# Result rows on adjacent partitions, brought together from two PSUM banks by two engines, at the end of an attention decode kernel

## The chip, the cores and the metric

The kernel runs on one core of one Trainium2 chip. The metric is the device time of one execution in microseconds. Most executions agree within 0.3%; all runs compared here are of the fast (undisturbed) state. The profile's span, from the first to the last instruction, is some 1.5 us shorter than that time. A page prints the span to 0.1 us; where hundredths are used below, they come from the trace itself (244.59 us before).

## The reference, cut to what matters

Two independent decode steps, A and B, each with one query token, 32 query heads, 16 key/value heads, head size 128. A attends to the last 2048 positions of its cache, B to all 8192. Each multiplies the joined heads (4096 values) with an output matrix `wo` and yields 576 numbers; the results are joined.

```python
def _B_ref(x, k_cache, v_cache, wq, wo):          # _A_ref: the same on the last 2048 positions
    q = (x @ wq).reshape(B, Sq, Hq, Dh).transpose(0, 2, 1, 3)
    k = jnp.repeat(k_cache, rep, axis=1)
    v = jnp.repeat(v_cache, rep, axis=1)
    p = _softmax(jnp.einsum("bhqd,bhkd->bhqk", q, k) * (Dh ** -0.5))
    o = jnp.einsum("bhqk,bhkd->bhqd", p, v)
    return o.transpose(0, 2, 1, 3).reshape(B, Sq, Hq * Dh) @ wo
# result: jnp.concatenate([a, b], axis=-1), 2 x 576 numbers in bf16
```

## The kernel before

Only the last step matters here. `wo` lies in SBUF as 32 rows of 576 columns on each of 128 partitions; the sum over 32 matmul steps, each contracting 128 partitions, gives the result. The 576 columns are dealt out over column groups of 32: two groups with 288 columns for A, four with 144 for B. Each group writes its own 32 PSUM partitions, of which one row is the result.

```python
DM = 576
OUTS = [2, 4]                       # column groups of A and of B
opj = nc.alloc_sbuf_tensor("opj", [128, 2, 64], BF16)         # columns 32.. are zero
outsb = nc.alloc_sbuf_tensor("outsb", [128, 2, DM // 2], BF16)
# ... ktps[0..3]: PSUM banks 0 to 3, 128 x 512 f32
def o_columns(P):
    add("dve", lambda dve: dve.tensor_copy(opj[:, P, 0:32], wsum[:, 272 + 32 * P:304 + 32 * P]),
        reads=[B_W], writes=[("opj", P)])
# ...
def wo_part(P, lo, n, off, res):
    def mm(pe):
        for jj in range(lo, lo + n):
            w = DM // OUTS[P]
            for j in range(OUTS[P]):
                o = off + (jj - lo) * DM + j * w
                ins = pe.matmul(ktps[P][32 * j:32 * j + 32, 0:w], lhsT=opj[:, P, jj:jj + 32],
                                rhs=slots[:, o:o + w], start=(jj == 0), stop=(jj == HQ - 1))
        return ins
    add("pe", mm, reads=[("opj", P)] + res, writes=[("bank", P)])

def finish_out(P):
    n = OUTS[P]
    add("dve", lambda dve: dve.tensor_copy(outsb[0:32 * n, P, 0:DM // n], ktps[P][0:32 * n, 0:DM // n]),
        reads=[("bank", P)], writes=[("outsb", P)])
    def put(eng):                   # n rows, 32 partitions apart
        src = bass.AP(tensor=outsb, offset=P * DM // 2, ap=[[32 * DM, n], [1, DM // n]])
        dst = out[0, 0:1, P * DM:(P + 1) * DM].rearrange("o (j n) -> (o j) n", j=n)
        return eng.dma_start(dst, src)
    add("sp", put, reads=[("outsb", P)], writes=[("out", P)], dma="out%d" % P)
# ... the last loads: wo of B in pieces of 21, 7, 3 and 1 rows; then for P in (0, 1): wo_part, finish_out
```

## Time and profile before

| | before |
|---|---|
| time, median of 3 (later of 6) | 246.19 (246.03) us |
| span | 244.6 us |
| bytes read | 102.76 MB at 420 GB/s |
| landings of the last two pieces of weights (3 rows, 1 row) | 241.87, 242.24 us |
| last matmul, copy, issue of the store end at | 242.56, 242.90, 243.49 us |

The kernel is a stream of loads with a serial tail. The prediction shows the lines of that tail, all but one: the weight loads of the last four matmuls wait once more, for the last row of weights.

```profile
242.29 0.10 PEld L690 LDWEIGHTS ktps<-slots,opj 128*32 128x32 bf16 x4 [0.19 <-DMA slots<-in_B_wo_dram]
```

The stretch after the last copy holds no instruction on a compute engine; it is read from windows of the trace. The columns are the stretch, its length, the busy time of the five engines, TensorE's clock, the share of the DMA engines' time that was busy, and GB/s. These are, of the kernel before: the issue of B's store (the time for which the profile shows its queue, `SPq` for SyncE, at work on it), the silence until its bytes, its bytes, and the rest to the end of the span.

```profile
242.92:243.50 0.58, 0.00 (x0) 0.00 (x0) 0.00 (x0) 0.00 (x0) 0.00 (x0) 1.00 0.00 0
243.50:244.13 0.63, 0.00 (x0) 0.00 (x0) 0.00 (x0) 0.00 (x0) 0.00 (x0) 1.00 0.00 0
244.13:244.22 0.09, 0.00 (x0) 0.00 (x0) 0.00 (x0) 0.00 (x0) 0.00 (x0) 1.00 0.08 13
244.22:244.59 0.37, 0.00 (x0) 0.00 (x0) 0.00 (x0) 0.00 (x0) 0.00 (x0) 1.00 0.00 0
```

The edges of windows are rounded to 0.01 us; by the trace the four take 0.57, 0.64, 0.09 and 0.36 us. From the start of the issue to the end of the span pass 1.66 us.

### The profile page before, as it was taken

Reading aid. Unit: us, or ns where it says so; the run is one execution under the profiler, and the core shown is the slowest. Engines: PE = TensorE matmul, PEld = TensorE weight load, DVE = VectorE, ACT = ScalarE, POOL = GpSimd, SP = SyncE. Lnnn points to the kernel's source line nnn. Section 1 sums busy time; section 2 is a strip of 40 time slices with the busy share of each in tenths; the row PEclk is TensorE's granted clock in tenths of the full one; section 3 lists DMA queues with packets and bytes.
Section 4 is the critical chain, followed back from the end, with each engine's and each line's share of the span. In section 5 each row is a group of like instructions: output and inputs, shape, how many; then the busy total and the mean of one; then the engine's idle time right before and its main releaser. Section 6 shows DMA issues by size and latency. Waiting matters only on the chain. (4 is left out here: it accounts for less than half of the span.)

```text
span 244.6 us, 5211 instructions
## 1 busy us (share of the span) xinstructions
PE 165.4 (68%) x2325; PEld 121.3 (50%) x2325; DVE 88.2 (36%) x152; ACT 92.7 (38%) x95; POOL 6.3 (3%) x33
## 2 busy tenths in 40 slices
PE   0007339968389995393999362999457799945965
PEld 0002139746236773233887221987232787624854
DVE  0001407864316454203556302455322246543031
ACT  2000016855306686102678300687600378630000
POOL 5000100000000000000000000000000000000000
PEclk9999957997759999569899859799957589975599
DMA  9999999999999999899999999999989999989993
GB/s 338 434 410 418 434 437 426 429 426 426 445 426 430 482 407 450 380 439 429 478 439 429 413 418 429 434 504 397 461 375 434 429 488 397 461 388 428 414 409 135
DMA packets 4068, 102.88 MB, mean 421 GB/s; under 512 B 602, under 2 KB 732, under 8 KB 988
## 3 DMA queue, kind: packets, MB, share of 16 engines
q1 hardware_dynamic: 3900, 102.76, 98.1%
q8 instruction: 6, 0.10, 0.2%
q10 hardware_dynamic: 160, 0.00, 0.0%
q14 instruction: 2, 0.02, 0.0%
HBM read 102.76 MB, written 0.00 MB: 420 GB/s over the span
## 5 line engine op out<-in xcount | busy, mean ns | idle before, releaser
L506 ACT ACTIVATE kt<-ktps 128x1024 bf16<-128x1024 bf16 x80 | 79.5, 1036 | 89.6 <-PE ktps L496 89.6
L496 PE MATMUL ktps<-ident,slots 128*128 128x128 bf16 x1280 | 87.8, 234 | 22.5 <-PEq L214 19.2
L496 PEld LDWEIGHTS ktps<-ident,slots 128*128 128x128 bf16 x1280 | 81.7, 106 | 38.0 <-issue 37.9
L509 DVE COPY kt<-ktps 128x1024 bf16<-128x1024 bf16 x80 | 60.7, 768 | 59.0 <-PE ktps L496 59.0
L588 PE MATMUL opsum<-slots,ptm 128*32 128x512 bf16 x320 | 28.5, 532 | 9.8 <-PEq L214 9.8
L521 PE MATMUL sacc<-kt,qst 128*32 128x512 bf16 x320 | 25.4, 392 | 2.2 <-PEq L214 2.2
L588 PEld LDWEIGHTS opsum<-slots,ptm 128*32 128x32 bf16 x320 | 14.0, 129 | 22.9 <-issue 20.6
L559 PE MATMUL misc<-ident,psb 128*128 128x128 bf16 x40 | 4.6, 285 | 15.8 <-PEq L214 15.8
L547 ACT ACTIVATE psb<-sacc,stat 128x2048 bf16<-128x2048 f32 x5 | 9.8, 1967 | 10.1 <-DVE stat L536 10.1
L606 DVE TENSOR_TENSOR vtmp<-opsum,maskV 128x512 f32<-128x512 f32 x4 | 2.8, 692 | 30.2 <-PE opsum L588 30.2
L559 PEld LDWEIGHTS misc<-ident,psb 128*128 128x128 bf16 x40 | 3.4, 125 | 18.2 <-issue 18.2
L438 PE MATMUL misc<-xnine,twice 64*128 64x18 bf16 x1 | 0.2, 170 | 18.0 <-DMA xnine<-in_B_x_dram 18.0
L566 DVE TENSOR_TENSOR ptm<-misc,maskP 128x1024 bf16<-128x1024 bf16 x5 | 3.5, 691 | 16.0 <-PE misc L559 16.0
L521 PEld LDWEIGHTS sacc<-kt,qst 128*32 128x32 bf16 x320 | 5.0, 94 | 8.3 <-issue 4.6
L438 PEld LDWEIGHTS misc<-xnine,twice 64*128 64x128 bf16 x1 | 0.1, 99 | 18.0 <-issue 18.0
L462 ACT ACTIVATE qrow<-opsum 128x512 bf16<-128x512 f32 x1 | 0.6, 597 | 19.4 <-PE opsum L456 19.4
L690 PE MATMUL ktps<-slots,opj 128*32 128x144 bf16 (+1 forms) x192 | 6.7, 247 | 0.7 <-issue 0.5
L690 PEld LDWEIGHTS ktps<-slots,opj 128*32 128x32 bf16 x192 | 5.3, 96 | 1.9 <-issue 0.6
L447 DVE TENSOR_SCALAR xpad<-misc,par 128x5 bf16<-128x5 f32 (+1 forms) x8 | 1.2, 229 | 13.8 <-PE misc L438 13.8
L481 POOL COPY qst<-qcol 128x32 bf16<-128x32 bf16 x8 | 1.7, 211 | 147.4 <-PE sacc L521 147.4
L559 PE MATMUL turned<-ident,psb 128*128 128x128 bf16 x40 | 5.3, 313 | 0.0
L534 DVE TENSOR_REDUCE stat<-sacc 128x1 f32<-128x512 f32 x5 | 3.5, 691 | 4.4 <-PE sacc L521 4.4
(75 smaller groups left out, 52.9 us busy)
## 6 DMA issues: line engine op xcount, KB each, us to landing
slots<-in_B_k_cache_dram SPq DMA_DIRECT2D x8, 4096.0 KB
slots<-in_A_k_cache_dram SPq DMA_DIRECT2D x4, 2048.0 KB
slots<-in_A_v_cache_dram SPq DMA_DIRECT2D x4, 2048.0 KB
slots<-in_A_wq_dram SPq DMA_DIRECT2D x1, 4608.0 KB, 13.8
slots<-in_B_wq_dram SPq DMA_DIRECT2D x1, 4608.0 KB, 24.0
slots<-in_A_wo_dram SPq DMA_DIRECT2D x1, 4608.0 KB, 18.7
slots<-in_B_wo_dram SPq DMA_DIRECT2D x1, 3024.0 KB, 25.5
slots<-in_B_wo_dram SPq DMA_DIRECT2D x1, 1008.0 KB, 7.7
```

Source lines behind the costliest of these rows:

```text
L481: return pool.tensor_copy(dst, src)
L496: ins = pe.matmul(ktps_bf[q][:, t * 128:(t + 1) * 128], lhsT=slots[:, o:o + 128], rhs=ident[:, :], start=True, stop=True, is_transpose=True)
L506: add("act", lambda act, src=src, dst=dst: act.activation(dst, src, ACT.Copy), reads=[("bank", q)], writes=[("kt", u % NKT, q)], tag="e%d% ...
L509: add("dve", lambda dve, src=src, dst=dst: dve.tensor_copy(dst, src), reads=[("bank", q)], writes=[("kt", u % NKT, q)], tag="e%d%d" % (u, q))
L521: ins = pe.matmul(sacc[32 * j:32 * j + 32, :], lhsT=qst[:, o:o + 32], rhs=rhs, start=(u == 0 and e == 0), stop=True, skip_group_check=True)
L534: add("dve", lambda dve: dve.tensor_reduce(st(C_M + g), sacc[:, :], AX.X, ALU.max), reads=[B_S], writes=[("st", C_M + g)], tag="max")
L547: return act.activation(dst, src, ACT.Exp, bias=st(C_NB + g), scale=SCALE, accum_out=st(C_L + g))
L559: ins = pe.matmul(dst[:, t * 128:(t + 1) * 128], lhsT=psb[:, o:o + 128], rhs=ident[:, :], start=True, stop=True, is_transpose=True)
L566: return dve.tensor_tensor(ptm[:, c * 1024:(c + 1) * 1024].rearrange("p (t y) -> p t y", t=8), dst.rearrange("p (t y) -> p t y", t=8), mas ...
L588: ins = pe.matmul(opsum[64 * j + 32 * x:64 * j + 32 * x + 32, :], lhsT=ptm[:, o:o + 32], rhs=v[:, at[0], at[1], :, :, b:b + 128], start=(n ...
L606: add("dve", lambda dve: dve.tensor_tensor(vtmp[:, :, :], src, by, ALU.mult), reads=[B_O, w], writes=["vtmp"], tag="keep")
L690: ins = pe.matmul(ktps[P][32 * j:32 * j + 32, 0:w], lhsT=opj[:, P, jj:jj + 32], rhs=slots[:, o:o + w], start=(jj == 0), stop=(jj == HQ - 1))
```

## The change

The intent is to let the store take two adjacent rows of 576 B in place of rows that lie 32 partitions apart. The result row of a column group falls on the partition that the place of the weight column in its 32-column window gives. The window of even groups is placed so that the result comes on the group's partition 31, that of odd groups so that it comes on the first, which is partition 32 of the pair. B has two such pairs of groups, each with half of a row's columns; the second pair writes another bank, and ScalarE copies it to partitions 31 and 32 while VectorE copies the first.

```diff
-    opj = nc.alloc_sbuf_tensor("opj", [128, 2, 64], BF16)
+    opj = nc.alloc_sbuf_tensor("opj", [128, 2, 96], BF16)
 ...
-        add("dve", lambda dve: dve.tensor_copy(opj[:, P, 0:32], ...
+        add("dve", lambda dve: dve.tensor_copy(opj[:, P, 31:63], ...
 ...
-                    o = off + (jj - lo) * DM + j * w
-                    ins = pe.matmul(ktps[P][32 * j:32 * j + 32, 0:w], lhsT=opj[:, P, jj:jj + 32],
+                    o = off + (jj - lo) * DM + j % 2 * (DM // 2) + j // 2 * w
+                    at = jj + j % 2 * 31
+                    ins = pe.matmul(ktps[P + j // 2][32 * j:32 * j + 32, 0:w], lhsT=opj[:, P, at:at + 32],
 ...
-        add("pe", mm, reads=[("opj", P)] + res, writes=[("bank", P)])
+        add("pe", mm, reads=[("opj", P)] + res, writes=[("bank", P + k) for k in range(P + 1)])
 ...
-        n = OUTS[P]
-        add("dve", lambda dve: dve.tensor_copy(outsb[0:32 * n, P, 0:DM // n], ktps[P][0:32 * n, 0:DM // n]),
-            reads=[("bank", P)], writes=[("outsb", P)])
- ... (put, shown above)
+        w = DM // OUTS[P]
+        for k, name in enumerate(("dve", "act")[0:P + 1]):
+            dst, src = outsb[0:64, P, k * w:(k + 1) * w], ktps[P + k][64 * k:64 * k + 64, 0:w]
+            add(name, lambda eng, k=k, dst=dst, src=src:
+                eng.activation(dst, src, ACT.Copy) if k else eng.tensor_copy(dst, src),
+                reads=[("bank", P + k)], writes=[("outsb", P, k)]).key = ("outsb", P)
+        add("sp", lambda sp: sp.dma_start(out[0, 0:1, P * DM:(P + 1) * DM].rearrange("o (j n) -> (o j) n", j=2),
+                                          outsb[31:33, P, :]),
+            reads=[("outsb", P, k) for k in range(P + 1)], writes=[("out", P)], dma="out%d" % P)
```

More of the change, by code (lines that the diff above doesn't have):

```diff
@@ L675, in o_columns @@
     def o_columns(P):
-        add("dve", lambda dve: dve.tensor_copy(opj[:, P, 0:32], wsum[:, 272 + 32 * P:304 + 32 * P]),
+        add("dve", lambda dve: dve.tensor_copy(opj[:, P, 31:63], wsum[:, 272 + 32 * P:304 + 32 * P]),
             reads=[B_W], writes=[("opj", P)])
@@ L688, in mm @@
                 for j in range(OUTS[P]):
-                    o = off + (jj - lo) * DM + j * w
-                    ins = pe.matmul(ktps[P][32 * j:32 * j + 32, 0:w], lhsT=opj[:, P, jj:jj + 32],
+                    o = off + (jj - lo) * DM + j % 2 * (DM // 2) + j // 2 * w
+                    at = jj + j % 2 * 31
+                    ins = pe.matmul(ktps[P + j // 2][32 * j:32 * j + 32, 0:w], lhsT=opj[:, P, at:at + 32],
                                     rhs=slots[:, o:o + w], start=(jj == 0), stop=(jj == HQ - 1))
             return ins
-        add("pe", mm, reads=[("opj", P)] + res, writes=[("bank", P)])
+        add("pe", mm, reads=[("opj", P)] + res, writes=[("bank", P + k) for k in range(P + 1)])
     def finish_out(P):
-        n = OUTS[P]
-        add("dve", lambda dve: dve.tensor_copy(outsb[0:32 * n, P, 0:DM // n], ktps[P][0:32 * n, 0:DM // n]),
-            reads=[("bank", P)], writes=[("outsb", P)])
-        def put(eng):
-            src = bass.AP(tensor=outsb, offset=P * DM // 2, ap=[[32 * DM, n], [1, DM // n]])
-            dst = out[0, 0:1, P * DM:(P + 1) * DM].rearrange("o (j n) -> (o j) n", j=n)
-            return eng.dma_start(dst, src)
-        add("sp", put, reads=[("outsb", P)], writes=[("out", P)], dma="out%d" % P)
+        w = DM // OUTS[P]
[7 more added lines that the diff above has]
+            reads=[("outsb", P, k) for k in range(P + 1)], writes=[("out", P)], dma="out%d" % P)
     WQ = [(4 * SLOT - WQ_W, [("v", 2)]), (SLOT, [("k", 1, 0), ("k", 1, 1), ("v", 0)])]
```

## The prediction

> **What bounds the kernel now.** I read the page's header and its part 2 first, to see which resource is full from end to end. Then the chain of waits over the last 20 us, which says what sets the end. Then the timeline of the last 2.5 us, because everything that the change edits lies there, and a few groups of instructions for durations.
>
> ```profile
> span 244.6 us, 5211 instructions
> ...
> PE 165.4 (68%) x2325; PEld 121.3 (50%) x2325; DVE 88.2 (36%) x152; ACT 92.7 (38%) x95; POOL 6.3 (3%) x33
> ...
> DMA  9999999999999999899999999999989999989993
> ...
> HBM read 102.76 MB, written 0.00 MB: 420 GB/s over the span
> ```
>
> The row DMA reads 9 (that is, 90% or more) or 8 in every slice but the last. No other engine is above 68%. The kernel streams 102.76 MB at 420 GB/s, and the transfers are the bound until the last weights have landed. Only the last slice (6 us) shows a 3: there the stream has run dry and a serial tail remains. The chain of waits gives the order of that tail (start, length, what):
>
> ```profile
> 233.52 8.35 DMA slots<-in_B_wo_dram
> 241.87 0.04 issue
> 241.92 0.65 PE ktps L690 x16
> 242.56 0.02 issue
> 242.59 0.31 DVE outsb L698
> ```
>
> The last four rows of B's output weights land at 241.87; 16 matmuls finish the sum by 242.56; one VectorE copy takes it out of PSUM. The timeline of the same stretch, and the one of A's result three microseconds earlier, show what follows a copy:
>
> ```profile
> 242.59 0.31 DVE L698 CAST outsb<-ktps 128x144 bf16<-128x144 f32 x1 [2.89 <-PE ktps L690]
> 242.92 0.57 SPq L704 DMA_DIRECT2D out_dram<-outsb  x1
> ```
> ```profile
> 239.25 0.45 DVE L698 CAST outsb<-ktps 64x288 bf16<-64x288 f32 x1 [3.62 <-PE ktps L690]
> 239.73 0.60 SPq L704 DMA_DIRECT2D out_dram<-outsb  x1
> ```
>
> B's copy ends at 242.59 + 0.31 = 242.90; SyncE takes up the store at 242.92 and is at it for 0.57 us, to 243.49. Windows of 0.05 us show the bytes of this store between 244.10 and 244.25, and the span ends at 244.6. So after the last matmul come 0.03 + 0.31 + 0.02 + 0.57 = 0.93 us of copying and issuing, about 0.61 us until the first bytes, some 0.15 us of bytes and some 0.35 us to the end: 2.04 us in all. That, plus at most the 0.65 us of matmuls, is all the change can reach: 2.7 of 244.6 us, 1.1%. A's store is issued 3.2 us before B's and is not on the path.
>
> The time outside is 246.19 us, 1.6 us more than the span; I carry that difference over unchanged.
>
> **What the Trainium skill says.** Four places bear on the edited operations.
>
> 1. "DMA: Bandwidth & Descriptors", section "Why a DMA increments its semaphore by 16 and not by 1": a store issued from SyncE uses the largest number of DMA engines up to 16 that divides the slowest dimension of both sides, and completion waits for each. B's store goes from four rows to two, so from four engines to two. The page of the kernel before does not list engines for this store, so nothing here confirms it.
> 2. Same page, "Latency and other measured facts": about 600 ns to the first byte for this kind of store. The trace agrees: 243.49 to 244.10 is 0.61 us. This part doesn't depend on the rows. The page's "Specifications" also says that pieces under 512 B cost a read-modify-write; the pieces grow from 288 B (144 elements of 2 B) to 576 B.
> 3. "ScalarE: Activation LUTs", section "What ACT_TABLE_LOAD costs": an activation with immediate scale and bias takes 186 ns + 0.833 ns per element of a row. For 512 elements that gives 612 ns; the trace has 597 for the 128x512 copy from PSUM, so it agrees to 3%. The section on table sets says that copies are in every set; the trace has a single table load of 1283 ns although copies and exponentials alternate, so no load of a table is to be feared.
> 4. "PSUM — Partial Sum Buffer", section "Specifications (TRN2)": ScalarE and VectorE may read PSUM side by side at full rate as long as their banks differ. The two copies read banks 1 and 2. No instruction of the kernel before shows two reads timed against each other, so I rely on the page here.
>
> **The change part by part.**
>
> The matmuls. The order of instructions on TensorE is the same in both kernels: 64 of 288 columns, 128 of 144 columns, each with a 32-column weight window. The window starts 31 columns later for odd column groups, which moves the result row from the group's first partition to partition 31 (even groups) or keeps it at the first (odd groups). Column groups 2 and 3 of B now write another bank. Nothing in count, size or wait changes: **0**.
>
> Clearing the weight buffer on GpSimd. 128x128 becomes 128x192. The 128x128 clear took 0.20 us and the 128x576 one 0.58, so 0.38 us per 448 columns, and 64 more columns cost about 0.05 us at 3.4 us into the run. TensorE's first matmul waits until 18.00 us for x by DMA and the work on VectorE that GpSimd releases is over at 4.4 us. Hidden: **0**.
>
> VectorE's copy for B. 128x144 becomes 64x144. The two old copies tell what a copy costs: both carry 18,432 elements, yet 64x288 took 450 ns and 128x144 took 307. So time goes by the columns (143 ns for 144 more, 0.99 ns each, on top of some 164 ns) and not by the partitions. Half the partitions save nothing: 307 ns remains, **0**.
>
> ScalarE's copy for B, new: 64x144 with partitions 64 to 127 as its source. From the page's formula 186 + 144 x 0.833 = 306 ns (an estimate). From this trace, between the 5-column activation of 208 ns and the 512-column copy of 597: 208 + 139 x 389/507 = 315 ns. From the copies of 512 and of 1024 columns (1036 ns): 597 - 368 x 0.857 = 282 ns. So 282 to 315 ns, side by side with VectorE's 307. ScalarE has been idle since 222.3 us, and took 0.03 us to react to VectorE there (222.10 to 222.13). It ends between 0.03 before and 0.01 us after VectorE: **0 to +0.02**. The split gains no copying time; it is there because two engines each bring one bank's half of each row to the same two partitions.
>
> The wait of SyncE. One semaphore counted to two by two engines instead of to one by VectorE. Reaction 0.02 us as before: **0**.
>
> The store of B. Two pieces of 576 B in place of four of 288 B. For the issue the trace has just these two forms: A's two pieces of 576 B took 0.60 us, B's four of 288 B took 0.57. B's store now has A's form, so the issue doesn't shrink: **-0.02 to +0.03**. The bytes: they are on the move for about 0.15 us, with staggered starts among engines; two engines in place of four, and no small pieces, may take 0 to 0.08 us off. The 0.35 us of receipt may shrink by up to 0.05 us because two completions have to come in and not four: together **-0.10 to 0**.
>
> The store of A has the same form (two pieces of 576 B), only from adjacent partitions, and is off the path: **0**.
>
> Sum: between -0.12 and +0.05 us, most likely -0.04. 246.19 - 0.04 = 246.15 us.
>
> **The rivals.**
>
> (a) *The split halves the copy.* If time went by elements, 0.31 us would become 0.16, and the kernel 246.03. Against it speak the two copies of equal element count above. For it: nothing.
>
> (b) *The small store was costly.* If a partial write of 288 B costs a read before the write, the bytes and receipt (0.5 us together) could lose 0.2 to 0.3 us: 245.9 to 246.0. For it: the page's 512 B. Against: the whole stretch from the first bytes to the end is 0.5 us, much of it fixed.
>
> (c) *ScalarE becomes the last.* It might start late, after 20 us of waiting outside its loop, or a read across partitions may be slow. At +0.1 to +0.3 us this makes 246.3 to 246.5. The reaction time of 0.03 us speaks against it; no earlier activation in the trace writes other partitions than it reads, so the doubt stays.
>
> (d) *The stream itself changes.* Other semaphores and a longer program could shift when loads start, and 1% of the stream is 2.4 us. But all loads stand in the same order behind the same waits, and everything edited but the clear comes after the last load was issued (234.4 us). I give it little.
>
> **Range and chances.** Every rival stays within 0.4 us, so the range is set by the repeat scatter, 245.87 to 246.22 in three runs of one kernel, plus the rivals: 245.7 to 246.6. A change beyond 2% is 4.9 us, nearly twice the 2.7 us that the edited tail lasts, so no mechanism of the change reaches it: faster 0.005, within 2% 0.99, slower 0.005.
>
> **What would show each step right or wrong.** The group of VectorE's copy at 64x144 should read 300 to 315 ns (rival a: 160 to 240), and ScalarE's new 64x144 row 280 to 320 ns, both starting within 0.05 us of the last matmul's end (rival c: ScalarE later or longer). The issue of B's store should take 0.55 to 0.62 us. From the end of issue to the end of the span should be 1.0 to 1.1 us, against 1.1 before; at 0.9 or less rival (b) is right. From the last matmul's end to the span's end should be 1.9 to 2.1 us. The landing of the last weights, which the change does not touch, may move by some tenths between any two runs, and that alone may decide the sign of the difference. A table load before ScalarE's copy, a gap in the row DMA before the last slice, or a time outside 244 to 248 us would prove my reading of the kernel wrong.

## The result, and the profile after

The changed kernel takes 245.47 us (median of 6 runs, 245.41 to 245.69), the kernel before 246.03 us in 6 runs (245.87 to 246.22). The ratio is 0.9978 with a 95% interval of 0.9966 to 0.9991. A ratio is the mean time of one kernel's fast runs over that of the other's fast runs of the same rounds, so it is not quite the ratio of the medians. The gain is 0.56 us of the medians: within 2%, but outside the predicted range of 245.7 to 246.6 us.

The page of the changed kernel, span and row of the DMA engines by slices:

```profile
span 244.0 us, 5212 instructions
...
DMA  9999999999999999899999999999989999989994
```

The stream is as full as before. The chain of waits of its last microseconds (start, length, what), and the timeline from the copies on:

```profile
231.89 9.93 DMA slots<-in_B_wo_dram
241.82 0.04 issue
241.87 0.64 PE ktps L691 x16
242.51 0.02 issue
242.53 0.30 DVE outsb L703
```
```profile
242.53 0.29 ACT L703 ACTIVATE outsb<-ktps 64x144 bf16<-64x144 f32 x1 [21.12 <-PE ktps L691]
242.53 0.30 DVE L703 CAST outsb<-ktps 64x144 bf16<-64x144 f32 x1 [4.46 <-PE ktps L691]
242.86 0.26 SPq L705 DMA_DIRECT2D out_dram<-outsb  x1
```

The landings (241.82 and 242.19 us against 241.87 and 242.24), the 16 matmuls (0.64 against 0.65) and the copy (0.30 against 0.31) hardly moved, and ScalarE's copy runs beside VectorE's. The last loads were released 1.6 us earlier in this execution than in the one before (231.89 against 233.52), and still landed at the same time, which fits DMA engines that are busy all the while (8 or 9 in the row DMA until the last slice). What moved is the issue of the store, from 0.57 to 0.26 us. The windows of the changed kernel, cut at the same events as those of before:

```profile
242.86:243.12 0.26, 0.00 (x0) 0.00 (x0) 0.00 (x0) 0.00 (x0) 0.00 (x0) 1.00 0.00 0
243.12:243.60 0.48, 0.00 (x0) 0.00 (x0) 0.00 (x0) 0.00 (x0) 0.00 (x0) 1.00 0.00 0
243.60:243.64 0.04, 0.00 (x0) 0.00 (x0) 0.00 (x0) 0.00 (x0) 0.00 (x0) 1.00 0.12 29
243.64:244.02 0.38, 0.00 (x0) 0.00 (x0) 0.00 (x0) 0.00 (x0) 0.00 (x0) 1.00 0.00 0
```

Line by line against before, by the trace's times: the issue -0.31 us, the silence after it -0.15, the bytes -0.05, the rest +0.01. Together 1.15 in place of 1.66 us: -0.51 us. With the 0.05 by which the last row landed earlier and 0.01 from there to the start of the issue it makes up the 0.57 us by which the spans differ.

The same shows in A's store, which is off the path: the prediction has it at 0.60 us in the kernel before; the changed kernel issued it in 0.29 us. A's store has two pieces of 576 B in both kernels. So neither the number nor the size of the pieces can be what made it quick, and the step between the rows became the theory to test. (The kernel before also writes its source pattern by hand, with `bass.AP`, where the changed kernel takes a slice; the first experiment rules that out.)

### The profile page after: what moved, and what is told of

It is laid out like the page before. It is cut to its first block, busy times and chain, and to the rows that moved or that the text cites. A ratio compares the mean times of both kernels' runs of the same rounds, so it can differ in the third digit from the quotient of the medians.

```text
span 244.0 us, 5212 instructions
## 1 busy us (share of the span) xinstructions
PE 165.8 (68%) x2325; PEld 120.5 (49%) x2325; DVE 88.2 (36%) x152; ACT 93.2 (38%) x96; POOL 6.4 (3%) x33
## 5 line engine op out<-in xcount | busy, mean ns | idle before, releaser
L588 PE MATMUL opsum<-slots,ptm 128*32 128x512 bf16 x320 | 27.4, 515 | 7.7 <-PEq L214 7.7
L588 PEld LDWEIGHTS opsum<-slots,ptm 128*32 128x32 bf16 x320 | 13.3, 125 | 20.3 <-issue 18.0
```

Of the source, the lines that this page charges most:

```text
L588: ins = pe.matmul(opsum[64 * j + 32 * x:64 * j + 32 * x + 32, :], lhsT=ptm[:, o:o + 32], rhs=v[:, at[0], at[1], :, :, b:b + 128], start=(n ...
```

## The experiments

Every experiment is the changed kernel with one edit, unless it says otherwise. They ran in three groups, each on a chip of its own, each beside runs of the kernel before: its medians there were 246.04, 246.03 and 246.06 us, so the three groups can be laid side by side.

**Theory S:** the partition step of the rows that the store reads sets how long its issue takes. **Rival P:** fewer and larger pieces. **Further questions:** what ScalarE and the second bank bring by themselves, and whether A's store counts.

### B's rows 32 partitions apart again

```diff
-                    at = jj + j % 2 * 31
+                    at = jj + 31 - ROWS[P][j % 2]          # B: rows 31 and 63; A: 31 and 32
 ...
-                                          outsb[31:33, P, :]),
+                                          bass.AP(tensor=outsb, offset=ROWS[P][0] * DM + P * DM // 2,
+                                                  ap=[[(32 + ROWS[P][1] - ROWS[P][0]) * DM, 2], [1, DM // 2]])),
```

> Only the place of B's result rows goes back to being 32 partitions apart (31 and 63 in place of 31 and 32); two pieces of 576 B, two banks, VectorE and ScalarE stay. Theory S (the step of partitions in the store's source sets the time of its issue): issue of B's store 0.57 to 0.60 us and a time near the kernel before, ratio 0.999 to 1.001. Rival P (fewer and larger pieces are what helps): issue about 0.26 us and ratio near 0.998. If the issue goes back to 0.57 but the time comes back only half, part of the gain belongs to the pieces' bytes and completion. Result right.

Measured: 245.98 us (245.92 to 246.13), ratio 1.0001 (0.9987 to 1.0014), result right. Its two stores, A's and B's, and the windows of B's, cut at the same events:

```profile
239.59 0.29 SPq L706 DMA_DIRECT2D out_dram<-outsb  x1
...
242.79 0.60 SPq L706 DMA_DIRECT2D out_dram<-outsb  x1
```
```profile
242.78:243.38 0.60, 0.00 (x0) 0.00 (x0) 0.00 (x0) 0.00 (x0) 0.00 (x0) 1.00 0.00 0
243.38:244.03 0.65, 0.00 (x0) 0.00 (x0) 0.00 (x0) 0.00 (x0) 0.00 (x0) 1.00 0.00 0
244.03:244.08 0.05, 0.00 (x0) 0.00 (x0) 0.00 (x0) 0.00 (x0) 0.00 (x0) 1.00 0.09 23
244.08:244.45 0.37, 0.00 (x0) 0.00 (x0) 0.00 (x0) 0.00 (x0) 0.00 (x0) 1.00 0.00 0
```

The whole gain is gone although two engines, two banks and two large pieces stay. The issue is back at 0.60 us, and the silence after it at 0.65; the bytes stay short (0.05). The four sum to 1.67 us, no better than the 1.66 of before. Here both stores write their source by hand, with two pieces of 576 B each: A's, at a step of one partition, took 0.29 us to issue, B's, at a step of 32, 0.60. So the way of writing isn't the cause. Theory S holds in this run, and fewer pieces without adjacency brought nothing that shows in the time.

### Only A's rows adjacent

The kernel before with A's rows on 31 and 32; B with four rows 32 apart, one bank and one copy.

```diff
-                    ins = pe.matmul(ktps[P][32 * j:32 * j + 32, 0:w], lhsT=opj[:, P, jj:jj + 32],
+                    at = jj + (31 if P else j * 31)
+                    ins = pe.matmul(ktps[P][32 * j:32 * j + 32, 0:w], lhsT=opj[:, P, at:at + 32],
 ...
-            src = bass.AP(tensor=outsb, offset=P * DM // 2, ap=[[32 * DM, n], [1, DM // n]])
+            src = bass.AP(...) if P else outsb[31:33, 0, :]
```

> Only A's store has its rows on partitions 31 and 32; B is as in the kernel before (four rows 32 apart, one bank, one copy by VectorE). Theory S and off the path: issue of A's store about 0.29 us, B's 0.57, ratio 0.9995 to 1.0005. Rival (A's shorter issue is what gained): ratio near 0.998. Result right.

Measured: 246.05 us (245.90 to 246.54), ratio 1.0001 (0.9987 to 1.0014), result right. A's issue took 0.28 us, B's 0.62. (The profiled execution is the one of 246.54 us; the other four lie between 245.90 and 246.07.) A's shorter issue brings nothing, as SyncE had to wait for B anyway. The gain is B's alone. A's store is therefore a free probe: a form can be tried on it without touching the end.

### Four pieces from the two adjacent partitions

B's rows stay on 31 and 32, but the two halves of a row lie 160 elements apart, so each row is two pieces of 288 B (the tile is widened for that).

```diff
-            dst, src = outsb[0:64, P, k * w:(k + 1) * w], ...
+            dst, src = outsb[0:64, P, k * 160:k * 160 + w], ...
 ...
-                                          outsb[31:33, P, :]),
+                return sp.dma_start(dst.rearrange("o (j k n) -> (o j) k n", j=2, k=2),
+                                    outsb[31:33, P, 0:320].rearrange("p (k n) -> p k n", k=2)[:, :, 0:w])
```

> B's store keeps the adjacent partitions 31 and 32 but moves four pieces of 288 B (a gap between the two halves of a row). Theory S: issue about 0.26 us and ratio 0.998 to 0.9985. Rival P: issue 0.5 us or more, first-to-last bytes about 0.15 us and ratio 0.9995 to 1.0005. Result right.

Measured: 246.20 us (246.10 to 246.34), ratio 1.0010 (0.9996 to 1.0024), result right. From the timeline, A's store and B's:

```profile
239.56 0.29 SPq L710 DMA_DIRECT2D out_dram<-outsb  x1
...
242.85 0.77 SPq L708 DMA_DIRECT2D out_dram<-outsb  x1
```

This was a miss for theory S: with adjacent partitions B's issue took 0.77 us, the longest of all. Either small pieces do cost (rival P), or something else in the form of this store does. In the built program its destination, which is contiguous, is folded to 4 x 144 elements while its source stays 2 x 2 x 144. The next runs take the readings apart.

### Other steps: B by 2, A by 8

The same edit as in the first experiment with rows 30 and 32 for B, 24 and 32 for A.

```diff
+ROWS = [(24, 0), (30, 0)]          # A: rows 24 and 32 + 0; B: rows 30 and 32 + 0
```

> As the changed kernel, but B's rows lie on partitions 30 and 32 (a step of 2) and A's on 24 and 32 (a step of 8). Theory S1 (any step other than one partition is slow): issue 0.57 to 0.62 us for both stores, first bytes about 1.2 us after the start of B's issue, ratio 0.9995 to 1.0005. Rival S2 (only large steps are slow, the time grows with the step): B's issue 0.26 to 0.35 us, A's between, ratio near 0.998. Result right.

Measured: 246.05 us (245.96 to 246.31), ratio 1.0003 (0.9990 to 1.0017), result right. A's store and B's in the timeline:

```profile
239.82 0.69 SPq L706 DMA_DIRECT2D out_dram<-outsb  x1
...
242.84 0.61 SPq L706 DMA_DIRECT2D out_dram<-outsb  x1
```

A step of 2 is as slow as one of 32 (0.61 against 0.60 us for two pieces of 576 B), so the issue doesn't grow with the distance: one partition is quick, any other tried step is slow. A's store, issued while loads are still running, took 0.69 us here at a step of 8, and 0.69 at 16 and at 4 in two runs below, a little more than its 0.60 at a step of 32. That small difference stays open.

### Four rows of 288 B on four adjacent partitions

The result is wrong on purpose: partitions 33 and 34 hold no result. A's rows lie on 16 and 32.

```diff
-              ...rearrange("o (j n) -> (o j) n", j=2), outsb[31:33, P, :]),
+              ...rearrange("o (j n) -> (o j) n", j=2 + 2 * P), outsb[31:35, P, 0:w] if P else bass.AP(...)),
```

> Wrong result on purpose: B's store takes four rows of 288 B from the adjacent partitions 31 to 34 (a plain two-dimensional form, step of one partition); A's rows on 16 and 32 (a step of 16). The run with four pieces from two adjacent partitions took 0.77 us to issue, which has two readings. Theory D (the form decides: rows at a step of one partition, without a further dimension, are quick, whatever their number): B's issue 0.26 to 0.30 us, first bytes 0.75 us after its start, ratio 0.998 to 0.9985. Rival P2 (pieces under 512 B or more than two of them are slow): B's issue 0.5 us or more, ratio near 1.000. A's issue 0.60 us by S1.

Measured: 245.51 us (245.43 to 245.82), ratio 0.9984 (0.9971 to 0.9998), result wrong as intended. A's store, B's copies and store:

```profile
237.49 0.69 SPq L706 DMA_DIRECT2D out_dram<-outsb  x1
...
242.84 0.30 SPq L706 DMA_DIRECT2D out_dram<-outsb  x1
```

Four pieces of 288 B, the very count and size of the kernel before, issue in 0.30 us when their rows step by one partition. The silence after it is 0.48 us and the bytes take 0.07. Rival P falls: against the changed kernel, four small pieces cost at most 0.05 us in the issue and 0.03 in the bytes.

### Four pieces from two partitions, with both sides in the same form

As in the run with 0.77 us, but the column blocks are dealt out so that a partition's two pieces are not neighbours in the destination either, and both sides keep the form 2 x 2 x 144. A's rows lie on 28 and 32.

```diff
-                    o = off + (jj - lo) * DM + j % 2 * (DM // 2) + j // 2 * w
+                    o = off + (jj - lo) * DM + (j * w if P else j * (DM // 2))
 ...
-                return sp.dma_start(dst.rearrange("o (j k n) -> (o j) k n", j=2, k=2), ...
+                return sp.dma_start(dst.rearrange("o (k j n) -> (o j) k n", j=2, k=2), ...
```

> B's store takes four pieces of 288 B from the adjacent partitions 31 and 32 as in the run that took 0.77 us to issue, but the column blocks are dealt out so that source and destination both keep the form 2x2x144 (there the destination had been folded to 4x144). If a further dimension is what is slow: issue 0.6 to 0.8 us, ratio 1.000 to 1.001. If the differing forms of the two sides were slow: 0.26 to 0.32 us, ratio 0.998 to 0.9985. A's rows lie on 28 and 32 (a step of 4), off the path: 0.6 to 0.7 us by the reading that any step but one is slow. Result right.

Measured: 245.60 us (4 runs, 245.32 to 245.71), ratio 0.9978 (0.9963 to 0.9993), result right. A's store and B's:

```profile
237.72 0.69 SPq L710 DMA_DIRECT2D out_dram<-outsb  x1
...
243.15 0.28 SPq L708 DMA_DIRECT2D out_dram<-outsb  x1
```

A further dimension is not slow: 0.28 us. What the run with 0.77 us had, and this one hasn't, is a source and a destination of different forms. So theory S needs a second clause: the quick issue was seen where the rows step by one partition and both sides have the same form.

### Both copies on VectorE

```diff
-        for k, name in enumerate(("dve", "act")[0:P + 1]):
+        for k, name in enumerate(("dve", "dve")[0:P + 1]):
```

(The copy is `tensor_copy` in both cases.)

> Both 64x144 copies of B on VectorE, one after the other; all else as in the changed kernel. Theory: the split does not shorten the copy against the kernel before, but with two copies on one engine the second comes on top: 0.30 us less an overlap, so +0.15 to +0.30 us against the changed kernel, ratio to before 0.9985 to 0.9995. Rival (the copies are hidden behind something): ratio stays 0.998. Result right.

Measured: 245.79 us (245.77 to 246.00), ratio 0.9994 (0.9981 to 1.0008), result right. The timeline shows the two copies and the store:

```profile
242.49 0.64 DVE L703 CAST outsb<-ktps 64x144 bf16<-64x144 f32 x2 [4.63 <-PE ktps L691]
243.16 0.26 SPq L705 DMA_DIRECT2D out_dram<-outsb  x1
```

The second copy comes fully on top: 0.64 in place of 0.30 us, and 245.79 - 245.47 = 0.32 us in time, at the upper end of what was expected. Of the adjacency's gain less than half is left. This is what ScalarE brings: not a shorter copy, but a second one at no cost.

### Two column groups, one bank, one engine

B is treated like A: two groups of 288 columns, rows on 31 and 32.

```diff
-OUTS = [2, 4]
+OUTS = [2, 2]
 ...
-        for k, name in enumerate(("dve", "act")[0:P + 1]):
+        for k, name in enumerate(("dve",)):
```

> The adjacent rows without the two banks and ScalarE: B uses two column groups of 288 columns like A, one bank, one copy of 64x288 by VectorE, rows on 31 and 32. Issue 0.26 us and first bytes 0.74 us after it starts, so 0.5 us off; the copy takes 0.45 in place of 0.31 us, so 0.15 us on; eight matmuls of 288 columns in place of sixteen of 144 after the last landing: -0.1 to +0.2 us. Together ratio 0.9985 to 0.9995, so worse than the changed kernel by 0.1 to 0.35 us. If it equals the changed kernel (0.998), the two banks and ScalarE bring nothing. Result right.

Measured: 245.71 us (245.55 to 245.87), ratio 0.9986 (0.9972 to 1.0000), result right.

```profile
242.68 0.45 DVE L703 CAST outsb<-ktps 64x288 bf16<-64x288 f32 x1 [4.80 <-PE ktps L691]
243.16 0.26 SPq L705 DMA_DIRECT2D out_dram<-outsb  x1
```

The issue is quick (0.26), the copy 0.15 us longer. Adjacency alone, without a second bank or ScalarE, gains 0.35 us over the kernel before (246.06 - 245.71), and the change's other half adds some 0.2 us to that. The intervals of the two ratios overlap, so this 0.2 is rough; the copy's length in the trace is firmer.

### A's result as a single piece

A's two halves are copied by VectorE and ScalarE to partition 0 and stored as one piece of 1152 B; B is as in the changed kernel.

```diff
-        for k, name in enumerate(("dve", "act")[0:P + 1]):
-            dst, src = outsb[0:64, P, k * w:(k + 1) * w], ktps[P + k][64 * k:64 * k + 64, 0:w]
+        for k, name in enumerate(("dve", "act")):
+            h = 64 if P else 32
+            dst, src = outsb[0:h, P, k * w:(k + 1) * w], ktps[P + k * P][h * k:h * k + h, 0:w]
 ...  # A stores outsb[0:1, 0, :] of 576 elements
```

> A's result is copied by VectorE and ScalarE to one partition and stored as a single piece of 1152 B; B as in the changed kernel. A's store is off the path and serves to measure the issue only. If a single row is issued quicker than two adjacent ones: under 0.25 us; by theory D it is also free of a further dimension and takes 0.25 to 0.30 us. Ratio as the changed kernel, about 0.998. Result right.

Measured: 245.47 us (4 runs, 245.38 to 245.54), ratio 0.9979 (0.9964 to 0.9995), result right. A's issue took 0.28 us, the same as for two adjacent rows (0.29). So a single row buys nothing over two adjacent ones, and there is no reason to bring B's result to one partition with more copies.

### B's store issued by ScalarE

```diff
-        add("sp", lambda sp: sp.dma_start(out[0, ...
+        add(("sp", "act")[P], lambda sp: sp.dma_start(out[0, ...
```

> As the changed kernel, but ScalarE's queue issues B's store, after its own copy and VectorE's. If the issue there takes 0.26 us as on SyncE: ratio 0.9975 to 0.998, 0 to 0.03 us better than the changed kernel. If issues on that queue are longer (its two loads of x took 0.54 and 0.61 us, though in another form): ratio 0.999 to 1.000. Result right.

Measured: 245.59 us (245.53 to 245.75), ratio 0.9985 (0.9971 to 0.9998), result right. The windows of the issue, the silence and the bytes:

```profile
242.77:243.28 0.51, 0.00 (x0) 0.00 (x0) 0.00 (x0) 0.00 (x0) 0.00 (x0) 1.00 0.00 0
243.28:243.53 0.25, 0.00 (x0) 0.00 (x0) 0.00 (x0) 0.00 (x0) 0.00 (x0) 1.00 0.00 0
243.53:243.57 0.04, 0.00 (x0) 0.00 (x0) 0.00 (x0) 0.00 (x0) 0.00 (x0) 1.00 0.12 29
```

The same store is shown as 0.51 us on ScalarE's queue and 0.26 on SyncE's, yet its bytes start 0.51 + 0.25 = 0.76 us after its start, nearly as on SyncE (0.26 + 0.48 = 0.74). So here the lengths of the issue on the two queues can't be compared, and the time from its start to the first bytes can. The Trainium skill, "Perfetto Trace Analysis", section "DMA Instruction — HWDGE (DVE, Sync)", says what that bar covers: from the moment when the semaphores are satisfied to the last excess increment of the completion semaphore, not the movement of data. In no run do the bytes lie inside it. The time is not better than the changed kernel's; that it is 0.1 us worse than that of the single-piece run on the same chip, though its span is as short, is left open.

## Why the prediction was wrong

**Right: where the kernel is bound and what the change can reach.** The stream is unchanged and the tail is what moved; the landing moved by 0.05 us. The whole effect stayed far inside 2%. Three readings were loose, without harm to the sum. At 241.87 us three of the last four rows landed, not all: the fourth came at 242.24, and the last four of the 16 matmuls waited for it. And the bytes of B's store began at 244.13 us, not 244.10, so the silence was 0.64 us. And one edited copy, that of A's weight columns at 228.13 us, comes before the last loads are issued; it took 0.19 us in both kernels.

**Right: the parts put at zero.** The last 16 matmuls take 0.64 against 0.65 us. VectorE's copy of 64x144 measured 299 ns, by columns and not by partitions, so rival (a) is out. ScalarE's measured 288 ns, within 282 to 315, and started with VectorE's, 0.02 us after the matmuls: rival (c) is out. No second table load shows in ScalarE's groups. A's store proved to be off the path.

**Wrong: the step "B's store now has A's form, so the issue doesn't shrink: -0.02 to +0.03".** It measured -0.31 us, the largest single term. The duration of A's store in the kernel before was taken as the price of two pieces of 576 B. But A's rows also lay 32 partitions apart there, and the price went with that. The prediction even noted that A's store would change "only" to adjacent partitions, and gave that word no cost. With B's rows moved apart again the whole gain is lost, and the run with a step of 2 shows that nearness doesn't help short of adjacency.

**Wrong: "This part doesn't depend on the rows", said of the time to the first byte.** On SyncE the silence after B's issue is 0.64 to 0.65 us in the five runs with a long issue and 0.48 to 0.49 in the six with a short one. This is a second term that moves with the first, -0.15 us.

**Right: bytes and receipt, -0.10 to 0.** The bytes measured -0.05; the rest, where the receipt lies, did not shrink (+0.01). The run with rows 32 apart kept the short bytes (0.05 us) and had no gain in time, as its issue and silence were each 0.01 to 0.03 us longer than before.

**The base.** The forecast of 246.15 us missed the 245.47 by 0.68 us. Of this, 0.16 is the base: the first three runs of the kernel before had a median of 246.19, all six one of 246.03. The other 0.52 is the change itself, -0.56 in place of -0.04.

**Rival (b) looked right and was not.** The test set for it was 0.9 us or less from the end of the issue to the end of the span, and the changed kernel shows 243.12 to 244.02, so 0.90. But the 0.2 to 0.3 us of rival (b) were to come from the bytes and the receipt, and these lost only 0.04; the rest came from the silence, which the test had included. And two runs with four pieces of 288 B at a step of one partition reach the short silence too, and nearly or wholly the changed kernel's ratio (0.9984 and 0.9978). The size of the pieces is not the cause.

**The number of DMA engines.** The prediction cited four engines becoming two and said that nothing confirmed it. The packet counts on the pages fit it: before, after, and the run whose source has two rows but whose destination four:

```profile
DMA packets 4068, 102.88 MB, mean 421 GB/s; under 512 B 602, under 2 KB 732, under 8 KB 988
```
```profile
DMA packets 4064, 102.88 MB, mean 422 GB/s; under 512 B 596, under 2 KB 728, under 8 KB 984
```
```profile
DMA packets 4066, 102.88 MB, mean 420 GB/s; under 512 B 600, under 2 KB 730, under 8 KB 986
```

The trace's records of single packets show one packet of 4 B for each engine that finishes: four of 288 B with four of 4 B before, two of 576 B with two of 4 B after. So four pieces on four engines become two pieces on two: 4 fewer packets in all, and under 512 B the four pieces and two completions, so 6 fewer. Both counts agree. The third run has its four pieces but two completions fewer, 4066 and 600. The four-row run has the 4068 and 602 of before, so four engines and pieces of 288 B, and is quick all the same.

**Overlooked: a mark that is set when the program is built.** The twelve kernels show a mark `ant_dge_precooked` on some of their transfers. Of their 24 result stores, the 15 whose rows step by one partition, or that have a single row, with both sides in one form, carry it, and the other nine don't. The 14 marked stores on SyncE took 0.26 to 0.30 us to issue, the nine unmarked ones 0.57 to 0.77. The loads on the same queue divide in the same way, in all twelve kernels: those of `wq` and `wo`, marked, took 0.33 to 0.44 us; those of keys and values, unmarked and with two sides of different form, 0.55 to 0.71. One group of each in the kernel before (the three numbers after the count are the shortest, median and longest issue in ns):

```profile
L407 SPq DMA_DIRECT2D slots<-in_B_k_cache_dram x8: 547/548/549, 45.9 to 172.7; - x8
L398 SPq DMA_DIRECT2D slots<-in_B_wo_dram x4: 327/432/441, 212.9 to 234.0; - x4
```

Two things follow. The prediction's "For the issue the trace has just these two forms" holds for stores alone: the same queue showed much shorter issues of loads, which could have warned. And no run here separates the form from the mark. What is shown is that the form decides whether the issue is quick; whether it does so by itself or only because the builder marks it, and why an unmarked transfer takes longer, stays open. The changed kernel, built without the marks, would decide.

## What to carry to other kernels

In this kernel the last store was paid in full, and its price depended on the form of its access pattern more than on its bytes: rows that step by one partition, with source and destination of the same shape, saved 0.5 us. The mark in the built program tells SyncE's quick transfers from its slow ones in all twelve kernels. Before the duration of one transfer is taken as the price of another, compare everything in the two forms, the partition step too. Where the window of a matmul's weight columns can be shifted, the partition of its result can be chosen; here this cost nothing in the matmuls (0.64 against 0.65 us), and a second engine brought the other half to the same partitions in the same time (0.29 us beside 0.30).

## What the Trainium skill lacked or had wrong

- "DMA: Bandwidth & Descriptors" says nothing of the partition step of a small store on SyncE. Two rows of 576 B were issued in 0.26 us at a step of 1 and in 0.60 to 0.61 at steps of 2 and 32 with the queues idle; beside running loads in 0.28 to 0.29 at a step of 1 and 0.60 to 0.69 at steps of 4, 8, 16 and 32.
- Nor does it say that two sides of different form are slow: 0.77 us for a source of 2x2x144 and a destination of 4x144, 0.28 with 2x2x144 on both (one run each).
- Same page, "Latency and other measured facts": about 600 ns to the first byte, without saying from which event. From the end of the issue of B's store it was 0.48 to 0.49 us in the quick form on SyncE, 0.25 on ScalarE's queue and 0.64 to 0.65 in the slow form; from its start 0.74 to 0.78 and 1.2 to 1.4.
- Same page, "Specifications", on pieces under 512 B: the section gives the cost no size. Four pieces of 288 B in the quick form took 0.03 and 0.07 us more than two of 576 B, from the start of the issue to the end of the span.
- No page says that the same store shows 0.51 us on ScalarE's queue and 0.26 on SyncE's while its bytes start 0.76 and 0.74 us after the start of the issue.
- No page has the mark `ant_dge_precooked` of the built program. SyncE's issues in the twelve kernels took 0.26 to 0.44 us with it and 0.55 to 0.77 without.
